# Attention and token/channel mixer on one core: Q, K and u transposed by the DMA crossbar instead of TensorE

## Chip, cores, metric

One core of a Trainium2 chip. The metric is device time in microseconds (us) of one execution; lower is better. Executions of the kernel before agree within 0.4%.

## The reference

Block-sparse attention over 4 batches x 8 heads x 768 positions x 64, then a token mixer and a channel mixer over x of 4 x 768 x 512:

```python
scores = scale * q @ k.T            # 768 x 768 per head
mask   = band | first/last block | 3 sampled blocks per row of blocks
attn   = softmax(where(mask, scores, -1e9)) @ v
x = attn, heads side by side        # B, S, 512
h = relu(x.T @ w_tok1) @ w_tok2     # along the 768 positions
u = x + h.T
out = u + relu(u @ w_ch1) @ w_ch2   # along the 512 channels, 1536 inside
```

## The kernel before

Heads go in pairs, 16 of them. A small planner inside the kernel keeps a clock for each engine, with booked costs, and writes the instructions down in the order of its plan. Each engine then runs its own list in that order and waits on semaphores. So a wait in one list stops all that stands behind it.

TensorE contracts over partitions, so Q and K (positions on partitions as loaded) must be turned, and so must u before the channel mixer. Before, both go over TensorE, PSUM and a copy:

```python
def transposes(p):                      # pair p: K, then Q
    ...
    for c in range(NC):                 # 6 chunks of 128 positions
        nc.tensor.matmul(out=box["t"][:, c, :], lhsT=lays[nm][:, c, :, :]..., rhs=ident,
                         is_transpose=True, ...)
    for hd in range(2):                 # one PSUM copy per head
        nc.vector.tensor_copy(out=buf[0:64, :], in_=i)      # or nc.scalar.copy
# rows 64 to 88 of every K and Q buffer hold the block mask; they are written once

def tok(b, g):                          # half g of the channels of batch b
    ... token mixer, u = x + h ...
    for dmc in (2 * g, 2 * g + 1):
        for sc in range(NC):
            nc.tensor.matmul(out=tbox["pt"][:, sc, :], lhsT=u[:, sc, 128 * dmc : ...],
                             rhs=ident, is_transpose=True, ...)
        nc.vector.tensor_copy(out=uT[:, dmc, :], in_=pt)    # or nc.scalar.copy

P.stream(0, qk_stream())    # scores, exponentials on ScalarE
P.stream(1, pv_stream())    # values, normalised by DVE
P.stream(2, tr_stream())    # transposes of Q and K
P.stream(3, tok_stream())
P.stream(4, ch_stream())    # channel mixer, lowest priority: fills what is left
```

Loads are issued by GpSimd, which casts float32 to bf16 on the way; Q, K and V of a pair are 128 partitions x 2 runs of 1536 bytes each.

The softmax here doesn't subtract the row's maximum and nothing guards it: scores larger than these inputs give would overflow.

## Time and profile before

| | before |
|---|---|
| time, median | 288.54 us (288.20 to 288.65, 4 runs) |
| span of the profiled run | 287.1 us |
| TensorE / ScalarE / DVE busy | 94% / 67% / 45% |
| first score matmul of pair 2 (the third pair) | 34.3 us |
| end of the last exponential | 160.9 us |
| from there to the end | 126.2 us |

The last three rows cut the span into a start, an attention stage and a channel stage.

### The profile page before, as it was taken

To read this page: it belongs to the slowest core of one execution; us is meant where nothing else is said; L and a number is where in the kernel's file an instruction comes from. 1 tells how busy PE (TensorE), PEld (TensorE's weight loads), DVE (VectorE), ACT (ScalarE), POOL (GpSimd) and SP (SyncE) were. 2 spreads that over 40 slices of the span, in tenths; PEclk is the share of its full clock that TensorE was granted. 3 is DMA by queue.
4 is the path that set the end of the run, shared out by engine and by line. 5 is a ranking of instruction groups with operands and counts; after the bars stand their busy time and mean duration, and the time that the engine had idled before them with its cause. 6 is when DMAs were issued, how large, how long until landed. Compare 5 with 4: busy or idle time off the path is not lost.

```text
span 287.1 us, 6351 instructions
## 1 busy us (share of the span) xinstructions
PE 269.9 (94%) x2682; PEld 175.5 (61%) x2690; DVE 130.2 (45%) x286; ACT 191.9 (67%) x286; POOL 45.0 (16%) x70
## 2 busy tenths in 40 slices
PE   0799899999999999999999999999999999999994
PEld 0366676678777777777777754456544654456441
DVE  5789966557777569765546341210022001200121
ACT  1589999999999999999999642037501770067200
POOL 7956554522211000000000000000000000000000
PEclk9999999999999999999999999999999999999999
DMA  4999999996254100000000001220022001210122
GB/s 55 134 204 202 214 201 205 201 185 87 39 73 66 23 2 2 0 2 3 2 0 2 2 0 39 106 76 0 2 110 84 29 0 73 94 54 0 38 102 82
DMA packets 19168, 20.07 MB, mean 70 GB/s; under 512 B 1348, under 2 KB 15428, under 8 KB 19140
## 3 DMA queue, kind: packets, MB, share of 16 engines
q0 software_dynamic: 15648, 13.37, 30.3%
q1 hardware_dynamic: 3492, 6.29, 5.8%
q8 instruction: 21, 0.34, 0.5%
q14 instruction: 7, 0.06, 0.1%
HBM read 26.74 MB, written 6.29 MB: 115 GB/s over the span
## 4 chain that ended last, share of the span: by engine, by line
PE 73%; ACT 14%; DVE 6%; issue 2%; DMA 2%; POOL 2%; POOLq 0%; DVEq 0%; ACTq 0%
PE pm_ch L686 22%; PE pm_ch L664 21%; ACT et L478 14%; PE ps L470 14%; PE po L520 8%; PE pm_tok L578 3%; PE pm_tok L603 2%; DMA kraw<-in_k_dram 2%; DVE qtb L439 1%; PE pm_ut L628 1%; PE tq L421 1%; DVE ktb L439 1%; PE tk L421 1%; DVE x L535 1%; DVE klay L394 1%
## 5 line engine op out<-in xcount | busy, mean ns | idle before, releaser
L478 ACT ACTIVATE et<-ps 128x768 bf16<-128x768 f32 x192 | 143.2, 810 | 4.2 <-PE ps L470 3.2
L470 PE MATMUL ps<-qtb,ktb 88*128 88x384 bf16 x384 | 95.3, 329 | 4.0 <-ACT et L478 1.7
L560 ACT ACTIVATE rc<-pm_ch 128x384 bf16<-128x384 f32 x84 | 41.2, 491 | 60.7 <-PE pm_ch L664 44.8
L520 PEld LDWEIGHTS <-et 128*128 128x128 bf16 x1152 | 56.0, 97 | 22.8 <-DVE x L535 1.9
L664 PE MATMUL pm_ch<-uT,w_ch 128*128 128x384 bf16 x384 | 68.6, 326 | 0.2 <-DVE rc L562 0.2
L686 PE MATMUL pm_ch<-w_ch,rc 128*128 128x512 bf16 x280 | 62.4, 379 | 0.4
L520 PE MATMUL po<-vaug,et 128*128 128x65 bf16 x1152 | 61.5, 193 | 0.5 <-ACT et L478 0.2
L694 DVE TENSOR_TENSOR o<-pm_ch,x 128x512 f32<-128x512 f32 x24 | 16.6, 692 | 98.7 <-PE pm_ch L686 98.7
L664 PEld LDWEIGHTS <-w_ch 128*128 128x128 bf16 x384 | 37.0, 98 | 23.1 <-issue 0.3
L686 PEld LDWEIGHTS <-rc 128*128 128x128 bf16 x288 | 28.2, 98 | 33.6
L470 PEld LDWEIGHTS <-ktb 88*128 88x128 bf16 x384 | 34.2, 99 | 11.9 <-issue 4.4
L439 DVE COPY ktb<-tk 64x768 bf16<-64x768 bf16 x29 | 16.0, 552 | 17.5 <-PE tk L421 17.2
L611 DVE TENSOR_TENSOR x<-pm_tok,x 128x512 bf16<-128x512 f32 x24 | 16.2, 687 | 6.8 <-PE pm_tok L603 6.5
L535 DVE TENSOR_TENSOR x<-po,recip 128x384 bf16<-128x384 f32 x32 | 17.8, 557 | 1.1
L439 DVE COPY qtb<-tq 64x768 bf16<-64x768 bf16 x30 | 16.6, 552 | 2.1 <-PE tq L421 1.1
L603 PE MATMUL pm_tok<-a_t,w_tok 128*128 128x256 bf16 x96 | 17.0, 272 | 0.0
L230 POOL DMA_DIRECT2D vraw<-in_v_dram x16 | 12.3, 766 | 28.4 <-DVE vaug L391 25.7
L578 PE MATMUL pm_tok<-x,w_tok 128*128 128x256 bf16 x96 | 16.3, 272 | 0.0
L230 POOL DMA_DIRECT2D kraw<-in_k_dram x16 | 11.6, 727 | 7.7 <-DVE recip L534 2.2
L230 POOL DMA_DIRECT2D qraw<-in_q_dram x16 | 11.5, 720 | 6.4 <-DMA w_ch<-in_moe_w_ch_dram 2.4
L534 DVE RECIPROCAL recip<-po 128x6 f32<-128x6 f32 x32 | 6.2, 195 | 12.0 <-PE po L520 11.6
L421 PE MATMUL tq<-ident,qlay 128*128 128x128 bf16 x96 | 11.3, 230 | 0.2 <-DVE qlay L394 0.2
(49 smaller groups left out, 122.8 us busy)
## 6 DMA issues: line engine op xcount, KB each, us to landing
out_dram<-o SPq DMA_DIRECT2D x24, 256.0 KB, 2.0
kraw<-in_k_dram POOLq DMA_DIRECT2D x16, 192.0 KB, 7.9
qraw<-in_q_dram POOLq DMA_DIRECT2D x16, 192.0 KB, 7.4
vraw<-in_v_dram POOLq DMA_DIRECT2D x16, 192.0 KB, 7.0
w_ch<-in_moe_w_ch_dram POOLq DMA_DIRECT2D x8, 384.0 KB, 9.8
w_tok<-in_moe_w_tok_dram POOLq DMA_DIRECT2D x1, 384.0 KB, 7.8
w_tok2r<-in_moe_w_tok_dram POOLq DMA_DIRECT2D x1, 384.0 KB, 9.0
samp<-in_sampled_blocks_dram SPq DMA_DIRECT2D x1, 0.6 KB
```

The costliest lines, as they stand in the source:

```text
L230: nc.gpsimd.dma_start(out=raw[:, :, :, :], in_=APx(src, 2 * p * S * D, [[NC * D, 128], [S * D, 2], [1, NC * D]]),)
L421: nc.tensor.matmul(out=box["t"][:, c, :], lhsT=lays[nm][:, c, :, :].rearrange("p h d -> p (h d)"), rhs=ident[:, :], start=(c == 0), stop=( ...
L439: nc.vector.tensor_copy(out=buf[0:64, :], in_=i)
L470: nc.tensor.matmul(out=ps[:, hd, 0:384], lhsT=ktb[n][0:88, 128 * j : 128 * j + 128], rhs=qtb[n][0:88, 384 * half : 384 * half + 384], star ...
L478: nc.scalar.activation(out=et[:, :, :], in_=ps[:, :, 0:384], func=AF.Exp, scale=0.125)
L520: nc.tensor.matmul(out=po[:, hd, c, :], lhsT=et[:, hd, 128 * c : 128 * c + 128], rhs=va[:, hd, j, 0:65], start=(j == 0 and hd == 0 and c = ...
L535: nc.vector.tensor_tensor(out=free(xs[b][:, 3 * half, 128 * pb : 128 * pb + 128], 0, [[64, 2], [DM, 3], [1, 64]]), in0=po[:, :, :, 0:64], ...
L560: nc.scalar.activation(out=o(), in_=i, func=AF.Relu)
L578: nc.tensor.matmul(out=box["pm"][:, t, :], lhsT=w_tok1[:, sc, 128 * t : 128 * t + 128], rhs=xs[b][:, sc, 256 * g : 256 * g + 256], start=( ...
L603: nc.tensor.matmul(out=ubox["pm"][:, i, :], lhsT=w_tok2[:, t, 2 * s2 + i, :], rhs=a_t[:, t, :], start=(i == 0 and t == 0), stop=(i == 1 an ...
L664: nc.tensor.matmul(out=pbox["pm"][:, 0:384], lhsT=w_ch1[:, dmc, 128 * cc : 128 * cc + 128], rhs=st[b]["uT"][:, dmc, 384 * sh : 384 * sh + ...
L686: nc.tensor.matmul(out=pbox["pm"][:, :], lhsT=box["rc"][:, cc, 128 * sc : 128 * sc + 128], rhs=w_ch2[:, cc, :], start=(cc == 0), stop=(cc ...
```

## The change

The intent: take 264 transposes off TensorE and their PSUM copies off DVE, and let the DMA crossbar turn the data from SBUF to SBUF. Cut to its core:

```diff
+    NPE = 2          # pairs that stay on TensorE
+    NL = 3           # wide tiles: 64 columns of data, 24 of mask, 40 zeros per head and chunk
+    wide = {(nm, n): sb1.tile([128, 2, NC, 128], BF16, ...) for n in range(NL) for nm in ("k", "q")}
...
+    def crossbar(p):
+        lays = relayout(p)           # raw -> wide[nm, p % NL][:, :, :, 0:64]
+        for nm, bufs, there in (("k", ktb, kT_there), ("q", qtb, qT_there)):
+            nc.sync.dma_start_transpose(
+                out=bufs[p % NV][:, :, :].rearrange("e h (c s) -> e (h c) s", c=NC),
+                in_=wide[nm, p % NL][:, :, :, :].rearrange("p h c e -> p (h c e)"))
+            ev = P.op(("sp",), {"sp": 1500.0}, deps, emit, prio=1, lat=2500.0)
     def transposes(p):
+        if p >= NPE:
+            crossbar(p)
+            return
...
+        nc.sync.dma_start_transpose(      # in tok(b, g), one per half batch
+            out=st[b]["uT"][:, g, :, :, :].rearrange("e c m p -> e (c m) p"),
+            in_=st[b]["u"][:, g, :, :].rearrange("p c e -> p (c e)"))
-        for dmc in (2 * g, 2 * g + 1):    # the 12 transposes and 2 copies of u
-            ...
```

The layouts of x, u and their transpose are changed to suit, and clears and mask copies for the wide tiles come in. The planner books 1.5 us for the issue of a transpose and 2.5 us from there to its landing.

More of the change, by code (lines that the diff above doesn't have):

```diff
@@ L64, in __init__ @@
         self.now = 0.0
-        self.free_at = {"pe": 0.0, "act": 0.0, "dve": 0.0}
+        self.free_at = {"pe": 0.0, "act": 0.0, "dve": 0.0, "sp": 0.0}
         self.streams = []
@@ L75, in stream, with op @@
         self.streams.sort(key=lambda s: (s[0], s[1]))
-    def op(self, engines, cost, deps, emit, prio=5, lat=60.0):
+    def op(self, engines, cost, deps, emit, prio=5, lat=60.0, tags=()):
         done = Ev()
-        self.ops.append((prio, self.count, engines, cost, deps, emit, done, lat))
+        self.ops.append((prio, self.count, engines, cost, deps, emit, done, lat, tags))
         self.count += 1
@@ L130, in step @@
             nxt.append(self.free_at["pe"])
-        for eng in ("act", "dve"):
+        for eng in ("act", "dve", "sp"):
             if self.free_at[eng] > self.now:
@@ L136, in step @@
             for o in self.ops:
-                prio, num, engines, cost, deps, emit, done, lat = o
+                prio, num, engines, cost, deps, emit, done, lat, tags = o
                 if eng not in engines:
@@ L141, in step @@
                     continue
-                t = self.when(deps)
+                t = self.when(deps, tags)
                 if t is None:
@@ L150, in step @@
             if best is not None:
-                prio, num, engines, cost, deps, emit, done, lat = best
+                prio, num, engines, cost, deps, emit, done, lat, tags = best
                 self.ops.remove(best)
@@ L208 @@
     vaug = [sb1.tile([128, 2, NC, 66], BF16, name=f"vaug{n}") for n in range(NV)]
-    qtb = [sb1.tile([128, S], BF16, name=f"qtb{n}") for n in range(2 * NV)]
-    ktb = [sb1.tile([128, S], BF16, name=f"ktb{n}") for n in range(2 * NV)]
+    qtb = [sb1.tile([128, 2, S], BF16, name=f"qtb{n}") for n in range(NV)]
+    ktb = [sb1.tile([128, 2, S], BF16, name=f"ktb{n}") for n in range(NV)]
+    wide = {
+        (nm, n): sb1.tile([128, 2, NC, 128], BF16, name=f"{nm}wide{n}")
+        for n in range(NL) for nm in ("k", "q")
+    }
     P = Planner({"ps": 2, "po": 1, "pm": 3, "et": NET, "a_t": 2, "o": 3, "rc": 2,
-                 "lay": 2, "kq": NV, "va": NV})
+                 "uT": 3})
     US = 1e3
@@ L324 @@
     indf = ind[R, :, :].rearrange("k c p -> k (c p)")
-    rows_there = {("k", n): Ev() for n in range(2 * NV)} | {("q", n): Ev() for n in range(2 * NV)}
+    rows_there = {(nm, n): Ev() for nm in ("k", "q") for n in range(2 * NPE)}
+    wide_there = {(nm, n): Ev() for nm in ("k", "q") for n in range(NL)}
     def mask_stream():
@@ L345, in copy @@
             def copy(eng, h=h):
-                nc.scalar.copy(out=qtb[0][R, 384 * h : 384 * h + 384], in_=pms[h][R, 0:384])
+                nc.scalar.copy(
+                    out=qtb[0][R, 0, 384 * h : 384 * h + 384], in_=pms[h][R, 0:384]
+                )
             e2.append(P.op(("act",), {"act": 420.0}, [done], copy, prio=0))
@@ L349, in mask_stream @@
         rows_there["q", 0].same_as = e2[1]
-        for n in range(2 * NV):
+        for n in range(2 * NPE):
             for nm, bufs in (("k", ktb), ("q", qtb)):
@@ L356, in copy @@
                     nc.vector.tensor_copy(
-                        out=bufs[n][R, :], in_=indf if nm == "k" else qtb[0][R, :]
+                        out=bufs[n // 2][R, n % 2, :], in_=indf if nm == "k" else qtb[0][R, 0, :]
                     )
@@ L367, with wide_stream, emit, clear @@
     ones_there = [Ev() for _ in range(NV)]
+    def wide_stream():
+        box, done, rel = {}, Ev(), Ev()
+        def emit():
+            P.take("pm", rel)
+            box["m"] = psM.tile([128, 2, NC, 24], FP32, tag="pm", name="pm_wide")
+            for i, rhs in enumerate((ident[R, 64:88], t2add[R, :])):
+                for c in range(NC):
+                    nc.tensor.matmul(
+                        out=box["m"][:, i, c, :], lhsT=ind[R, c, :], rhs=rhs,
+                        start=(i == 0 and c == 0), stop=(i == 1 and c == NC - 1),
+                    )
+        yield 500.0, [Ev(12.5 * US)], [("pm", 1)], emit, done
+        for n in range(NL):
+            for i, nm in enumerate(("k", "q")):
+                def clear(eng, nm=nm, n=n):
+                    nc.vector.memset(wide[nm, n][:, :, :, 64:128], 0.0)
+                def copy(eng, nm=nm, n=n, i=i):
+                    nc.vector.tensor_copy(
+                        out=wide[nm, n][:, :, :, 64:88],
+                        in_=free(box["m"][:, i, 0, :], 0, [[0, 2], [24, NC], [1, 24]]),
+                    )
+                ev = P.op(("dve",), {"dve": 420.0}, [], clear, prio=6)
+                ev = P.op(("dve",), {"dve": 450.0}, [done, ev], copy, prio=6)
+                wide_there[nm, n].same_as = ev
+                rel.same_as = ev
     START = 6.5 * US
@@ L391, in emit @@
                     nc.vector.tensor_copy(out=vaug[p % NV][:, :, :, 0:64], in_=raw[:, :, :, :])
-                    return
-                lay = sbw.tile([128, NC, 2, D], BF16, tag=f"{nm}lay", bufs=2, name=f"{nm}lay{p}")
-                nc.vector.tensor_copy(
-                    out=lay[:, :, :, :], in_=raw[:, :, :, :].rearrange("p h c d -> p c h d")
-                )
-                lays[nm] = lay
+                elif p >= NPE:
+                    nc.vector.tensor_copy(out=wide[nm, p % NL][:, :, :, 0:64], in_=raw[:, :, :, :])
+                else:
+                    lay = sbw.tile([128, NC, 2, D], BF16, tag=f"{nm}lay", bufs=1, name=f"{nm}lay{p}")
+                    nc.vector.tensor_copy(
+                        out=lay[:, :, :, :], in_=raw[:, :, :, :].rearrange("p h c d -> p c h d")
+                    )
+                    lays[nm] = lay
             deps = [arr]
@@ L401, in relayout @@
                 deps.append(pv_done[p - NV])
-            if nm != "v" and p >= 2:
-                deps.append(qT_there[p - 2, 1])
+            if nm != "v" and 1 <= p < NPE:
+                deps.append(qT_there[p - 1, 1])
+            if nm != "v" and p >= NPE:
+                deps.append(wide_there[nm, p % NL])
+                if p - NL >= NPE:
+                    deps.append(xb_done[nm, p - NL])
             lays[nm + "ev"] = P.op(("dve",), {"dve": 320.0}, deps, emit, prio=2 if nm != "v" else 3)
@@ L407, in relayout, with emit @@
         return lays
+    xb_done = {}
+    def crossbar(p):
+        lays = relayout(p)
+        for nm, bufs, there in (("k", ktb, kT_there), ("q", qtb, qT_there)):
+            def emit(eng, nm=nm, bufs=bufs):
+                nc.sync.dma_start_transpose(
+                    out=bufs[p % NV][:, :, :].rearrange("e h (c s) -> e (h c) s", c=NC),
+                    in_=wide[nm, p % NL][:, :, :, :].rearrange("p h c e -> p (h c e)"),
+                )
+            deps = [lays[nm + "ev"]]
+            if p >= NV:
+                deps.append(qk_done[p - NV])
+            ev = P.op(("sp",), {"sp": 1500.0}, deps, emit, prio=1, lat=2500.0)
+            xb_done[nm, p] = ev
+            there[p, 0], there[p, 1] = ev, ev
     def transposes(p):
+        yield lambda: ("v", p) in raws
+        if p >= NPE:
+            crossbar(p)
+            return
         for hd in range(2):
             kT_there[p, hd], qT_there[p, hd] = Ev(), Ev()
-        yield lambda: ("v", p) in raws
         lays = relayout(p)
@@ L425, in emit, with evac @@
                     )
-                deps = [lays[nm + "ev"]]
-                if p >= NV:
-                    deps.append(qk_done[p - NV])
-                yield 56.0, deps, [("pm", 1)] if c == 0 else [], emit, last if c == NC - 1 else None
-            n_left = [2]
+                yield 56.0, [lays[nm + "ev"]], [("pm", 1)] if c == 0 else [], emit, last if c == NC - 1 else None
             for hd in range(2):
-                buf = bufs[2 * (p % NV) + hd]
-                def evac(eng, hd=hd, buf=buf, box=box):
+                def evac(eng, hd=hd, buf=bufs[p % NV], box=box):
                     i = box["t"][64 * hd : 64 * hd + 64, :, :].rearrange("p c s -> p (c s)")
                     if eng == "act":
-                        nc.scalar.copy(out=buf[0:64, :], in_=i)
+                        nc.scalar.copy(out=buf[0:64, hd, :], in_=i)
                     else:
-                        nc.vector.tensor_copy(out=buf[0:64, :], in_=i)
+                        nc.vector.tensor_copy(out=buf[0:64, hd, :], in_=i)
                 ev = P.op(("dve", "act"), {"dve": 550.0, "act": 740.0}, [last], evac, prio=2)
@@ L468, in emit @@
                 for hd in range(2):
-                    n = 2 * (p % NV) + hd
+                    n = p % NV
                     nc.tensor.matmul(
-                        out=ps[:, hd, 0:384], lhsT=ktb[n][0:88, 128 * j : 128 * j + 128],
-                        rhs=qtb[n][0:88, 384 * half : 384 * half + 384], start=True, stop=True,
+                        out=ps[:, hd, 0:384], lhsT=ktb[n][0:88, hd, 128 * j : 128 * j + 128],
+                        rhs=qtb[n][0:88, hd, 384 * half : 384 * half + 384],
+                        start=True, stop=True,
                     )
@@ L489, in qk_stream @@
                 326.0,
-                [e for hd in range(2) for e in (
-                    kT_there[p, hd], qT_there[p, hd],
-                    rows_there["k", 2 * (p % NV) + hd], rows_there["q", 2 * (p % NV) + hd],
+                [e for hd in range(2) for e in [kT_there[p, hd], qT_there[p, hd]] + (
+                    [rows_there["k", 2 * p + hd], rows_there["q", 2 * p + hd]] if p < NPE else []
                 )],
@@ L531, in norm @@
                     if b not in xs:
-                        xs[b] = sbw.tile([128, NC, DM], BF16, tag="x", bufs=B, name=f"x{b}")
+                        xs[b] = sbw.tile([128, 2, NC, 256], BF16, tag="x", bufs=B, name=f"x{b}")
                     recip = sbw.tile([128, 2, 3], FP32, tag="recip", name=f"recip{p}_{half}")
@@ L535, in norm @@
                     nc.vector.tensor_tensor(
-                        out=free(xs[b][:, 3 * half, 128 * pb : 128 * pb + 128], 0,
-                                 [[64, 2], [DM, 3], [1, 64]]),
+                        out=free(
+                            xs[b][:, pb // 2, 3 * half, 128 * (pb % 2) : 128 * (pb % 2) + 128], 0,
+                            [[64, 2], [256, 3], [1, 64]],
+                        ),
                         in0=po[:, :, :, 0:64],
@@ L579, in emit @@
                         out=box["pm"][:, t, :], lhsT=w_tok1[:, sc, 128 * t : 128 * t + 128],
-                        rhs=xs[b][:, sc, 256 * g : 256 * g + 256],
+                        rhs=xs[b][:, g, sc, :],
                         start=(t == 0 and sc == 0), stop=(t == 1 and sc == NC - 1),
@@ L585, in tok @@
         if b not in st:
-            st[b] = dict(u=xs[b], uT_there=[Ev() for _ in range(4)])
+            st[b] = dict(u=xs[b], uT_there=[Ev() for _ in range(4)], uT_rel=Ev())
         a_rel = Ev()
@@ L611, in add @@
                 nc.vector.tensor_tensor(
-                    out=st[b]["u"][:, 2 * s2 : 2 * s2 + 2, 256 * g : 256 * g + 256],
-                    in0=ubox["pm"][:, :, :],
-                    in1=xs[b][:, 2 * s2 : 2 * s2 + 2, 256 * g : 256 * g + 256], op=ALU.add,
+                    out=st[b]["u"][:, g, 2 * s2 : 2 * s2 + 2, :], in0=ubox["pm"][:, :, :],
+                    in1=xs[b][:, g, 2 * s2 : 2 * s2 + 2, :], op=ALU.add,
                 )
@@ L620, in tok, with turn @@
         alias(a_rel, last)
-        for dmc in (2 * g, 2 * g + 1):
-            last, rel, tbox = Ev(), Ev(), {}
-            for sc in range(NC):
-                def emit(sc=sc, dmc=dmc, rel=rel, tbox=tbox):
-                    if sc == 0:
-                        P.take("pm", rel)
-                        tbox["pt"] = psM.tile([128, NC, 128], BF16, tag="pm", name=f"pm_ut_{b}_{dmc}")
-                    nc.tensor.matmul(
-                        out=tbox["pt"][:, sc, :], lhsT=st[b]["u"][:, sc, 128 * dmc : 128 * dmc + 128],
-                        rhs=ident[:, :], start=(sc == 0), stop=(sc == NC - 1), is_transpose=True,
-                    )
-                yield 56.0, [u_evs[sc // 2]], [("pm", 1)] if sc == 0 else [], emit, last if sc == NC - 1 else None
-            def evac(eng, dmc=dmc, tbox=tbox):
-                if "uT" not in st[b]:
-                    st[b]["uT"] = sbw.tile([128, 4, S], BF16, tag="uT", bufs=B, name=f"uT{b}")
-                o, i = st[b]["uT"][:, dmc, :], tbox["pt"][:, :, :].rearrange("p c s -> p (c s)")
-                if eng == "act":
-                    nc.scalar.copy(out=o, in_=i)
-                else:
-                    nc.vector.tensor_copy(out=o, in_=i)
-            ev = P.op(("dve", "act"), {"dve": 555.0, "act": 740.0}, [last], evac, prio=3)
-            alias(rel, ev)
+        def turn(eng):
+            if g == 0:
+                P.take("uT", st[b]["uT_rel"])
+                st[b]["uT"] = sbw.tile([128, 2, NC, 2, 128], BF16, tag="uT", bufs=3, name=f"uT{b}")
+            nc.sync.dma_start_transpose(
+                out=st[b]["uT"][:, g, :, :, :].rearrange("e c m p -> e (c m) p"),
+                in_=st[b]["u"][:, g, :, :].rearrange("p c e -> p (c e)"),
+            )
+        ev = P.op(("sp",), {"sp": 1500.0}, u_evs, turn, prio=2, lat=2500.0,
+                  tags=[("uT", 1)] if g == 0 else [])
+        for dmc in (2 * g, 2 * g + 1):
             alias(st[b]["uT_there"][dmc], ev)
@@ L665, in emit @@
                             out=pbox["pm"][:, 0:384], lhsT=w_ch1[:, dmc, 128 * cc : 128 * cc + 128],
-                            rhs=st[b]["uT"][:, dmc, 384 * sh : 384 * sh + 384],
+                            rhs=st[b]["uT"][:, dmc // 2, 3 * sh : 3 * sh + 3, dmc % 2, :],
                             start=(dmc == 0), stop=(dmc == 3),
@@ L678, in ch @@
                 rc_there[cc, sh] = ev
+        alias(st[b]["uT_rel"], last)
         for sc in range(NC):
@@ L694, in fin @@
                 nc.vector.tensor_tensor(
-                    out=o[:, :], in0=pbox["pm"][:, :], in1=st[b]["u"][:, sc, :], op=ALU.add
+                    out=o[:, :].rearrange("p (g e) -> p g e", g=2),
+                    in0=pbox["pm"][:, :].rearrange("p (g e) -> p g e", g=2),
+                    in1=st[b]["u"][:, :, sc, :], op=ALU.add,
                 )
@@ L733 @@
     P.stream(-1, mask_stream())
+    P.stream(-1, wide_stream())
     tok2_op = P.op(("dve",), {"dve": 900.0}, [tok2_raw], wtok2_lay, prio=3)
```

## The prediction

> **What bounds the kernel now.** I read the page first (slices, chain, groups), then a table of stretches, then the TensorE timeline in one of them, and last the landing times of the loads.
>
> ```profile
> PE   0799899999999999999999999999999999999994
> DVE  5789966557777569765546341210022001200121
> ACT  1589999999999999999999642037501770067200
> DMA  4999999996254100000000001220022001210122
> ...
> 70.00:99.00 29.00, 28.96 (x413) 22.23 (x410) 19.76 (x45) 28.75 (x39) 5.01 (x7) 1.00 0.41 57
> 99.00:126.00 27.00, 27.00 (x378) 20.42 (x376) 19.30 (x45) 26.90 (x37) 0.00 (x0) 1.00 0.01 2
> ```
>
> One slice is 7.2 us. Up to about 160 us (attention) TensorE and ScalarE are both full: 39 exponentials in 29 us and 37 in 27 us, one per 0.73 to 0.74 us (columns of a stretch: its length, then busy us and count of PE, weight loads, DVE, ACT, POOL; then clock, DMA share, GB/s). After that only TensorE is full. DVE has room, except before 35 us. The 16 DMA engines are full until about 65 us and nearly idle afterwards.
>
> ```profile
> 106.24 0.49 PE L470 MATMUL ps<-qtb,ktb 88*128 88x384 bf16 x2
> 106.57 0.34 PE L520 MATMUL po<-vaug,et 128*128 128x65 bf16 x6
> 106.75 0.39 PE L421 MATMUL tk<-ident,klay 128*128 128x128 bf16 x4
> 106.97 0.49 PE L470 MATMUL ps<-qtb,ktb 88*128 88x384 bf16 x2
> ```
>
> This is one step of attention, 0.73 us from score matmul to score matmul: scores 0.33, values 0.18, and 0.22 us left, here filled with four transposes (0.055 us each when pipelined). The filler place holds whatever the order gives it: transposes of K, Q and u, token mixing, or channel matmuls (L664). ScalarE sets the pace, TensorE fits exactly. Work taken out of the filler therefore does not shorten a step. It shortens the kernel only if channel matmuls of the last stage move into the place.
>
> ```profile
> 189.61 15.60 PE pm_ch L664 x96
> 205.48 10.74 PE pm_ch L686 x49
> 216.27 4.48 PE pm_ch L686 x20
> ```
>
> From the chain in order of time: the last stage is TensorE alone, 15.60/96 = 0.1625 us per L664 matmul, (10.74+4.48)/72 = 0.211 per L686 one.
>
> **What the Trainium skill says.** "TensorE: Matmul & The Clock Gate", Part 4, gives about 275 ns for a TensorE transpose in a kernel, and notes that its output needs a copy out of PSUM. The trace has 230 ns as latency of one, but only 0.055 us as spacing; the copies are the 0.55 us DVE rows below. "DMA: Bandwidth & Descriptors", section "Latency and other measured facts", gives 261 GB/s for a DMA transpose with a non-contiguous middle dimension and about 350 to 400 GB/s if contiguous; nothing in this trace shows one. The same page, "Queues, rings and completion order": each DMA engine takes turns between its queues, packet by packet. So transposes share with the loads, which here read float32 at twice the 200 GB/s that they write, about 400 GB/s (the page's "Specifications" put the ceiling at 435). The TensorE page, Part 1, calls DVE's queue strictly first in, first out; nothing in the trace contradicts it, and the argument on loads below rests on it.
>
> **The change, part by part.**
>
> *Removed from TensorE.* 14 pairs x 12 = 168 transposes and 96 of u: 264 x 0.055 = 14.5 us; 12 tiny matmuls come in. In the built orders, 39 L664 matmuls stand before the last score matmul in the old kernel; in the new one 96 and 6 of the second channel layer do. After the last score matmul it thus has 57 x 0.1625 + 6 x 0.211 + 12 x 0.055 = 11.2 us less to do. That is the gain if attention keeps its pace. The old pace from the third pair on is (160.9 - 35.0)/168 = 0.750 us per step; at 0.74 another 1.7 us goes. Best case: 288.56 - 11.2 - 1.7 = 275.7 us.
>
> *Removed from DVE and ScalarE.*
>
> ```profile
> L439 DVE COPY ktb<-tk 64x768 bf16<-64x768 bf16 x29 | 16.0, 552 | 17.5 <-PE tk L421 17.2
> L421 PE MATMUL tq<-ident,qlay 128*128 128x128 bf16 x96 | 11.3, 230 | 0.2 <-DVE qlay L394 0.2
> ```
>
> Some 56 + 16 PSUM copies of 0.55 us, about 40 us, nearly all DVE's. DVE limits nothing after 35 us, so this counts early only. There the copies for pairs 2 and 3 (8 x 0.55) and their mask rows (8 x 0.37), 7.4 us, give way to six clears and six mask copies of the new wide tiles (estimate 0.4 to 0.7 us each from the memset and copy rows, 5 to 7 us). Even.
>
> *Added: 36 crossbar transposes* of 128 x 1536 bf16, 393 KB each: 28 for K and Q, 8 for u. In the steady state one pair per 8.8 us needs two, and half of one for u, so 3.5 us is allowed for each. At 261 to 400 GB/s (skill) one takes an estimated 1.0 to 1.5 us of all engines. Not a bound late, when the DMA is idle.
>
> *Early it is different.* All transposes for pairs 2 to 7 fall before 75 us, where the loads fill the DMA. Two things can wait:
> First, pair 2. Its scores began at 34.6 us before. In the new order its Q is fifth on SyncE's queue, behind K and Q of pair 3 and K of pair 4, since its wide tile is cleared last; its copy stands in DVE's order behind Q of pair 4, which landed at 26.9 us. So it is issued at about 29 us, and lands near 34 to 36: no gain, perhaps a loss of some us.
> Second, DVE's order. In the old kernel the copies of raw K and Q were held back by lay buffers and from pair 6 on came 2 to 23 us after the data. In the new order they stand as early as the data was planned to come: K and Q of pairs 6 and 7 ahead of the normalising of pair 2's second half, of 8 and 9 ahead of pair 4's first, of 10 and 11 ahead of pair 5's first. If a load is late, DVE stands at its copy, the one PSUM tile of the values is not emptied, TensorE stops, and so does attention.
>
> ```profile
> L230 POOL DMA_DIRECT2D qraw<-in_q_dram x1: 713/713/713, 46.5 to 46.5; - x1
> ...
> DMA to landing us min/median/max: 10.1/10.1/10.1
> ```
>
> Issue plus time to landing, taken so for each: Q of pair 7 landed at 43.0 us, 9 at 56.6, 11 at 62.5, without transposes. With pair 2 at 34.6 and 0.74 us a step, pair 5's first half is normalised at 34.6 + 42 x 0.74 + 1.5 = 67.2. By then 14 transposes have had their turn (K, Q of six pairs, two of u). With x us of full DMA each, Q of pair 11 comes at 62.5 + 14x, and attention is delayed by 14x - 4.7. (The places at pairs 7 and 9 give 8x - 1.6 and 11x - 2, no more.) For x = 0.98 (the loads' own 400 GB/s) that is 9.0 us, for 1.5 16.3, for 0.5 2.3. After pair 11 the loads are slow enough for the DMA to keep up.
>
> Sum for x = 0.98: 275.7 + 9.0 = 284.7 us, rounded to 285.
>
> **The rivals.**
> 1. *The transposes hide wholly*: packets of transposes slip between those of the loads at little cost. For it: the DMA share over 1 says that packets overlap in one engine, and their source is not HBM. Against it: the loads move a steady 200 GB/s at any mix, which looks like a ceiling. Then 275 to 278 us.
> 2. *The loads come late and DVE stalls*, as in my sum: 280 to 292 us.
> 3. *The transposes themselves are slow*, in issue or in transfer. At over 3.5 us each they set the pace: at 5 us, 36 x 5 = 180 us from 24 us on puts the end of attention past 195 instead of 160, and the time above 300 us. Nothing in the trace speaks against it, as there is no transpose in it; the skill's figures do.
>
> **Range and chances.** Over 2% faster means under 282.8 us, that is x below about 0.85, or rival 1; 2% slower means over 294.3, x above about 1.65, or rival 3. I give rival 1 and small x 0.42, the middle 0.38, slow transposes 0.20. Range 275 to 298 us.
>
> **What will show it.** L664 matmuls before the last score matmul: 96, and about 110 us from it to the end instead of 127.3. The K and Q transposes' time to landing: 3 to 5 us early, 3 late. DVE waits for kraw and qraw, a few us each between 40 and 75 us, where there was 0.5 in all. The DMA full until 80 us or so, not 65. Pair 2 starting at 34 to 36 us. If DVE shows no wait for loads, my second step is wrong and it is about 276; if steps after 80 us take over 0.76 us with TensorE waiting for ktb or qtb, the transposes are the bound.

## More of the kernel before

Every run here is of state fast, or a single run of a one-core program, for which no state is given.

One more line of the page of before is needed for comparison: what the DMA engines carried.

```profile
DMA packets 19168, 20.07 MB, mean 70 GB/s; under 512 B 1348, under 2 KB 15428, under 8 KB 19140
...
q0 software_dynamic: 15648, 13.37, 30.3%
```

Queue 0 is GpSimd's (loads). Few packets are under 512 bytes.

## The result, and the profile after

The changed kernel takes 330.16 us median (329.07 to 331.62, 4 runs): 14.5% slower, ratio 1.1448 with a 95% interval of 1.1395 to 1.15. Ratios are the mean time of one kernel's fast runs over that of the other's of the same rounds, so not quite the ratio of the medians quoted.

| | before | after | difference |
|---|---|---|---|
| span | 287.1 | 329.9 | +42.8 |
| first score matmul of pair 2 | 34.3 | 69.2 | +34.8 |
| from there to the end of the last exponential | 126.6 | 146.9 | +20.4 |
| from there to the end | 126.2 | 113.8 | -12.4 |

The hoped-for gain is there, in the last row. Ahead of it 55.2 us are lost, more than four times as much. The slices of the page of after (one is 8.2 us):

```profile
PE   1798000069499669979999999999999999999995
...
PEclk9999755559879959997999999999999999999999
DMA  3999999995989977995636320215101200130022
```

TensorE stands still from slice 5 to 8, then has smaller holes up to slice 18. The granted clock falls with the holes. The chain of work that ended last, in order of time (start, length, what), names them:

```profile
30.58 13.23 SPq L461
43.86 17.63 DMA ktb<-kwide
61.48 7.55 DMA qtb<-qwide
69.17 1.44 PE ps L530 x4
...
79.34 8.97 DMA uT<-x
...
108.44 9.75 DMA uT<-x
```

The SPq and DMA lines are all crossbar transposes. SyncE's timeline has each one (SPq is SyncE's queue; start, time to issue, and x2 where two are merged):

```profile
23.82 6.70 SPq L461 DMA_TRANSPOSE ktb<-kwide  x1
30.58 13.23 SPq L461 DMA_TRANSPOSE qtb<-qwide  x1
43.86 17.58 SPq L461 DMA_TRANSPOSE ktb<-kwide  x2
61.48 5.76 SPq L461 DMA_TRANSPOSE qtb<-qwide  x2
...
150.57 1.42 SPq L461 DMA_TRANSPOSE ktb<-kwide  x1
152.04 1.77 SPq L461 DMA_TRANSPOSE qtb<-qwide  x1
```

The same instruction takes 1.4 to 1.8 us late and up to 13.2 us early. The first four landed 21.3, 22.8, 19.1 and 13.6 us after their issue began. Pair 2 needs the fifth of them. And the DMA engines are not idle or slow meanwhile; two stretches of 9 us in the middle of the hole (length, busy us and count of PE, weight loads, DVE, ACT, POOL; clock, DMA share, GB/s):

```profile
44.00:53.00 9.00, 0.00 (x0) 0.00 (x0) 0.00 (x0) 0.00 (x0) 3.71 (x5) 0.50 1.25 194
53.00:62.00 9.00, 0.00 (x0) 0.00 (x0) 0.00 (x0) 0.00 (x0) 0.00 (x0) 0.50 1.23 194
```

Nothing computes, and 194 GB/s are moved. The view of the DMA for 44 to 53 us splits them by queue (packets, MB, share of engine time; queue 1 carries the transposes):

```profile
q0 software_dynamic: 1601, 1.33, 91.0%
q1 hardware_dynamic: 1597, 0.40, 33.6%
```

The two queues get one packet each in turn, but a packet of the loads has some 830 bytes as written (1.33 MB/1601) and one of the transposes some 250. That is about 148 GB/s for the loads, which had 203 in the same stretch before, and 45 for the transposes. Six transposes of 393 KB landed between 23.8 and 70.1 us, which is 51 GB/s. The page counts what they are made of:

```profile
DMA packets 75616, 34.20 MB, mean 104 GB/s; under 512 B 57797, under 2 KB 71877, under 8 KB 75589
```

36 transposes of 128 x 12 rows of 256 bytes are 55,296 packets under 512 bytes, about what came in.

My theory from this (theory 1 in the expectations): a transpose is quick alone; beside loads its small packets take turns with large ones of the load queue, so it gets few bytes for its turns. The rivals: A, the order on SyncE's queue, where Q of pair 2 stands fifth; B, transposes are slow of themselves when several are in flight; C, the crossbar, not the size of the packets, gives way to loads.

### The profile page after: what moved, and what is told of

It is laid out like the page before. It is cut to its first block, busy times and chain, and to the rows that moved or that the text cites. A ratio compares the mean times of both kernels' runs of the same rounds, so it can differ in the third digit from the quotient of the medians.

```text
span 329.9 us, 5871 instructions
## 1 busy us (share of the span) xinstructions
PE 266.0 (81%) x2429; PEld 166.9 (51%) x2438; DVE 102.5 (31%) x234; ACT 184.0 (56%) x270; POOL 45.2 (14%) x70
## 4 chain that ended last, share of the span: by engine, by line
PE 71%; DMA 16%; SPq 4%; ACT 4%; DVE 3%; issue 1%; POOL 1%; POOLq 0%; DVEq 0%; ACTq 0%
PE pm_ch L714 19%; PE pm_ch L737 19%; PE ps L530 17%; PE po L580 9%; DMA uT<-x 6%; DMA ktb<-kwide 5%; DMA qtb<-qwide 5%; SPq L461 4%; PE pm_tok L665 3%; ACT et L539 3%; PE pm_tok L640 3%; PE tk L487 0%; DVE x L673 0%; DVE x L595 0%; DVE eq L320 0%
## 5 line engine op out<-in xcount | busy, mean ns | idle before, releaser
L530 PE MATMUL ps<-qtb,ktb 88*128 88x384 bf16 x384 | 101.2, 348 | 9.3 <-DMA qtb<-qwide 4.6
L714 PE MATMUL pm_ch<-uT,w_ch 128*128 128x384 bf16 x384 | 73.7, 329 | 9.4 <-DMA uT<-x 9.4
L580 PEld LDWEIGHTS <-et 128*128 128x128 bf16 x1152 | 59.3, 100 | 27.9 <-issue 5.4
L530 PEld LDWEIGHTS <-ktb 88*128 88x128 bf16 x384 | 37.1, 103 | 60.8 <-issue 49.0
L622 ACT ACTIVATE rc<-pm_ch 128x384 bf16<-128x384 f32 x72 | 35.3, 490 | 55.9 <-PE pm_ch L714 55.8
L580 PE MATMUL po<-vaug,et 128*128 128x65 bf16 x1152 | 64.2, 197 | 2.8 <-DVE x L595 2.3
L640 PE MATMUL pm_tok<-x,w_tok 128*128 128x256 bf16 x96 | 17.1, 285 | 31.1 <-DVE x L595 31.1
L624 DVE TENSOR_SCALAR rc<-pm_ch 128x384 bf16<-128x384 f32 x24 | 13.3, 555 | 20.9 <-PE pm_ch L714 20.8
L236 POOL DMA_DIRECT2D vraw<-in_v_dram x16 | 12.4, 776 | 53.8 <-DVE vaug L430 36.9
L595 DVE TENSOR_TENSOR x<-po,recip 128x384 bf16<-128x384 f32 x32 | 17.8, 557 | 1.1
L432 DVE COPY kwide<-kraw 128x768 bf16<-128x768 bf16 x14 | 5.1, 371 | 37.1 <-DMA ktb<-kwide 37.1
L236 POOL DMA_DIRECT2D kraw<-in_k_dram x16 | 11.7, 729 | 27.4 <-DVE recip L594 12.8
L640 PEld LDWEIGHTS <-w_tok 128*128 128x128 bf16 x96 | 8.0, 101 | 2.1 <-issue 0.3
```

Source lines behind the costliest of these rows:

```text
L236: nc.gpsimd.dma_start(out=raw[:, :, :, :], in_=APx(src, 2 * p * S * D, [[NC * D, 128], [S * D, 2], [1, NC * D]]),)
L530: nc.tensor.matmul(out=ps[:, hd, 0:384], lhsT=ktb[n][0:88, hd, 128 * j : 128 * j + 128], rhs=qtb[n][0:88, hd, 384 * half : 384 * half + 38 ...
L580: nc.tensor.matmul(out=po[:, hd, c, :], lhsT=et[:, hd, 128 * c : 128 * c + 128], rhs=va[:, hd, j, 0:65], start=(j == 0 and hd == 0 and c = ...
L595: nc.vector.tensor_tensor(out=free(xs[b][:, pb // 2, 3 * half, 128 * (pb % 2) : 128 * (pb % 2) + 128], 0, [[64, 2], [256, 3], [1, 64]],), ...
L622: nc.scalar.activation(out=o(), in_=i, func=AF.Relu)
L640: nc.tensor.matmul(out=box["pm"][:, t, :], lhsT=w_tok1[:, sc, 128 * t : 128 * t + 128], rhs=xs[b][:, g, sc, :], start=(t == 0 and sc == 0) ...
```

## The experiments

### 1. No loads beside the transposes

```diff
-                load_pair(x, max(evs))          # pairs 4 to 15
+                raws[nm, x] = kept[nm, x % NR]  # use the tiles of pairs 0 to 3 again
-            nc.gpsimd.dma_start(out=w_ch1[:, i, :], ...)     # and w_ch2
+            nc.gpsimd.memset(w_ch1[:, i, :], 0.04)
```

> The changed kernel in the same order, but Q, K and V of pairs 4 to 15 are not loaded (the tiles of pairs 0 to 3 are used again) and the two channel weights are filled with constants by GpSimd: wrong on purpose, and no load is in flight after about 25 us. Theory 1 (a transpose is fast alone, 1.4 us to issue, and slow only while loads share the DMA engines): every transpose takes 1.4 to 1.8 us to issue and lands in under 5 us, pair 2 starts at 31 to 34 us, the time is 272 to 279 us. Rival A (order on the SyncE queue, Q of pair 2 fifth, and heads of queue that wait): pair 2 still late and the time above 300 us. Rival B (a transpose is slow of itself when several are in flight): the early ones still take 6 us and more each.

286.38 us, against 330.16 with the loads. Its output is wrong, which doesn't matter for the time. SyncE's timeline, the same first transposes:

```profile
26.33 1.49 SPq L458 DMA_TRANSPOSE ktb<-kwide  x1
27.89 1.84 SPq L458 DMA_TRANSPOSE qtb<-qwide  x1
29.77 3.64 SPq L458 DMA_TRANSPOSE ktb<-kwide  x2
```

Same order of the plan, same transposes, 44 us less: rivals A and B cannot carry the loss. But my number was 272 to 279, and some waits stayed: pair 2 begins at 38.8 us, and the chain of work that ended last has a further 5.4 us of u at 48 us and 5.7 us of Q of a later pair at 69 us. Landing takes 3.7 to 4.3 us (medians) even alone, and more behind another transpose, while the plan has what depends on it close behind. Experiment 6 tests this remainder.

### 2. Pair 2 first in the queue

```diff
-    wide[nm, p % NL]
+    wide[nm, (p - NPE) % NL]      # in three places
```

> Only the order: pair p uses wide tile (p-2) mod 3 instead of p mod 3, so K and Q of pair 2 are cleared, copied and transposed first. Theory 1: each of them still takes some 9 us beside the loads, so pair 2 starts at about 45 to 50 us instead of 69, but each further pair costs another 18 us of transposes while loads last, and the time is 300 to 325 us. Rival A (order is the cause): pair 2 starts at 30 to 36 us and the time falls to 275 to 290 us.

328.35 us (one look): about as before the edit. Pair 2 now starts at 51.6 us instead of 69.2, but its Q still landed 26.2 us after its issue began, and the next pair waits again until 69.95 us. The order was poor, but it is not the cause. Rival A falls.

### 3 and 4. Each half of the change alone

```diff
     # e3: u back on TensorE, K and Q by the crossbar
+    XU = ()                  # batches whose u the crossbar turns
     # e4: K and Q of all pairs on TensorE, u by the crossbar
+    NPE = 16; XU = (0, 1, 2, 3)
```

> Half of the change undone: u is transposed on TensorE as before, K and Q of pairs from the third on by the crossbar. Theory 1: pair 2 as late as in the changed kernel (about 69 us), the two waits for u of 9 to 10 us fall away, 5 us of TensorE work comes back: 312 to 325 us. If the u transposes were what holds up the queue: below 300 us.

> The other half undone: K and Q all on TensorE as before, u of all batches by the crossbar. Theory 1: the first u (near 50 us, beside loads) lands some 9 us after its issue and holds TensorE up for up to that long once, the later ones lie under slack; TensorE has 5.3 us less: 283 to 292 us, so within 2% of before. Rival B: several waits for u of 5 to 10 us each: above 295 us.

K and Q alone: 319.68 us (one look), inside what theory 1 said; pair 2 starts at 70.8 us. From there to the end of the last exponential it takes 129.4 us instead of 146.9, so most of what the change loses after pair 2 comes with u. u alone: 295.96 us (295.37 to 296.21), ratio 1.0257, interval 1.0237 to 1.0276. That is 4 us above my range for it, and just above the edge that I gave to rival B, but there is one wait and not several: the first u, issued at 40.3 us among loads, landed 14.4 us later.

```profile
54.69 0.80 PE L751 MATMUL pm_ch<-uT,w_ch 128*128 128x384 bf16 x2 [9.74 <-DMA uT<-x]
```

The two matmuls for which TensorE waited belong to the work of lowest priority. They stand in the list ahead of the next scores, so the scores wait too. After the hole the granted clock is 0.50 (55 to 60 us), and a step's two score matmuls take 0.83 us there instead of 0.48. The halves cost 31.4 and 7.6 us, together 39.0; the whole costs 41.6.

### 5. The cost by itself

A kernel with no compute: two transposes, or two plain copies of the same 393 KB inside SBUF, beside a stream of GpSimd loads in runs of a chosen length.

```python
nc.gpsimd.dma_start(out=raw[i], in_=APx(base, at, [[run, 128], [128 * run, m], [1, run]]))  # x22, 11 of the longest
nc.sync.dma_start_transpose(out=d, in_=wsrc)                 # "turn", x2
nc.sync.dma_start(out=d[:, :, 0:128], in_=wsrc[:, :, :])     # "short": 256-byte runs
nc.sync.dma_start(out=d, in_=wsrc)                           # "long": one run of 3072 bytes
```

> The disputed cost by itself, output wrong on purpose. Stages with a barrier between them: two crossbar transposes of 128 x 1536 bf16 alone; the same two beside GpSimd loads of float32 in runs of 1536 bytes (as Q, K and V), 256, 512, 3072 and 6144 bytes; then two plain copies of the same 393 KB inside SBUF beside loads in runs of 1536 bytes, in runs of 256 bytes and of 3072 bytes; and both copies alone. Theory 1a (the DMA engines take turns packet by packet, so a 256-byte packet of a transpose waits for one load packet each time): the transpose takes some 1.5 us alone, 3 us beside 256-byte runs, 8 to 10 us beside 1536, 13 to 16 us beside 3072 and over 20 us beside 6144 (unless large runs are cut); the plain copy in 256-byte runs is as slow as the transpose, in 3072-byte runs 2 to 4 us. Rival C (the crossbar itself yields to loads, or shares by bytes): the same time beside all run lengths, and both plain copies fast.

The first try (257.0 us) was spoilt: the instructions were moved between stages, so that the stage without loads met loads. The second kept the written order.

> The cost by itself again, with the written order kept: in the first try the scheduler moved loads and stores between the stages, so that the stage without loads met loads (15.8 and 20.4 us to landing), and the one named 1536 bytes met none (3.7 and 4.0). Stages in order: two transposes alone; beside loads in runs of 1536, 256, 512, 3072, 6144 bytes; two plain copies of 393 KB beside 1536-byte loads in runs of 256 bytes, then of 3072 bytes; both alone. From the first try, theory 1a (turns by packet) expects to landing of the second: alone 4 us; beside 1536 about 17 to 21; beside 256 and 512 8 to 12, less than beside 1536; beside 3072 and 6144 17 to 40; plain copy in 256-byte runs 15 to 21, in 3072-byte runs under 8. Rival C (the crossbar itself): the plain copy in 256-byte runs lands in under 8 us beside loads.

287.15 us, a time that means nothing here. The three stages that decide (a number in a name is the load's run in float32 elements, so 384 is 1536 bytes; lines: issue, then time to landing):

```profile
L88 SPq DMA_TRANSPOSE dturn384x<-wsrc x2: 4295/5860/7424, 33.5 to 37.8; - x2
DMA to landing us min/median/max: 13.2/15.1/16.9
...
L91 SPq DMA_DIRECT2D dshort384x<-wsrc x2: 693/2290/3887, 200.9 to 201.7; - x2
DMA to landing us min/median/max: 13.2/16.8/20.4
...
L93 SPq DMA_DIRECT2D dlong384x<-wsrc x2: 493/1098/1703, 231.7 to 232.2; - x2
DMA to landing us min/median/max: 8.0/8.5/8.9
```

| transfer of 393 KB | beside loads in runs of | us to landing, first and second of the two |
|---|---|---|
| transpose | none | 3.9, 4.2 |
| transpose | 256 B | 8.9, 12.5 |
| transpose | 512 B | 9.9, 12.4 |
| transpose | 1536 B | 13.2, 16.9 |
| transpose | 3072 B | 18.4, 23.3 |
| transpose | 6144 B | 20.7, 14.1 |
| plain copy, 256-byte runs | 1536 B | 13.2, 20.4 |
| plain copy, 3072-byte runs | 1536 B | 8.0, 8.9 |
| plain copy, 256-byte runs | none | 3.5, 3.7 |
| plain copy, 3072-byte runs | none | 2.6, 2.8 |

A plain copy in 256-byte pieces is as slow beside loads as a transpose (medians 16.8 and 15.1 us); in 3072-byte pieces it takes about half as long (8.5). Longer runs of the load make the first transpose of a stage slower throughout, from 8.9 to 20.7 us. The second one beside 6144 bytes, 14.1 us, is no exception: that stage has 11 loads, which had ended by 191.8 us, and from then to 194.5 us 1593 of the two transposes' 3072 packets moved. So the size of the packets on both sides sets it, and rival C falls: nothing special to the crossbar is needed.

The DMA view of stretches in which both queues had work shows the turns themselves, packets of loads against packets of the transfer: 2727 and 2739 (39 to 53 us, runs of 1536 bytes), 1998 and 1997 (143 to 159 us, 3072), 902 and 945 (178 to 191 us, 6144), and for the plain copy in 256-byte runs 2751 and 2712 (207 to 221 us). That is one for one, as in the changed kernel. Only beside runs of 256 bytes is it not so all the time (2645 and 504 from 72 to 75 us); why, stays open. Each stage was run once.

### 6. Without loads, with a later booking

```diff
-    wide[nm, p % NL] ... {"sp": 1500.0} ... lat=2500.0
+    wide[nm, (p - NPE) % NL] ... {"sp": 2000.0} ... lat=8000.0
```

> The changed kernel without the late loads once more (wrong on purpose), with 8 us instead of 2.5 booked by the planner between issue and landing of a transpose, and pair 2 first in the wide tiles. Without loads 286.4 us was measured, with waits left at pair 2 (38.8 us), u (5.4 us) and Q (5.7 us). If these come from an order planned for a landing that is too early, they go: 272 to 279 us. If they come from the queue being full of transposes, they stay: 283 us and more.

280.59 us (one look), between the two answers: 5.8 us of the remainder of experiment 1 was order, two edits together. What stays is in part the start, where transposes are needed as soon as they can be issued: pair 2 begins at 37.2 us even here, and at 34.1 us in experiment 7, which leaves the first pairs on TensorE.

### 7 and 8. The crossbar only after the loads

```diff
-    NPE = 2
+    NPE = 8                 # 10 in the other
+    XU = (1, 2, 3)          # u of batch 0 stays on TensorE
-    ... [Ev(12.5 * US)] ... # set-up of the wide tiles
+    ... [Ev(40 * US)] ...
     # booking 2 and 8 us, wide tile (p - NPE) % NL, mask rows in all four K/Q buffers
```

> A version meant to keep the gain: crossbar for K and Q of pairs 8 to 15 and u of batches 1 to 3 only, the rest on TensorE as before; the planner books 8 us instead of 2.5 from the end of issue to landing, so that copies which wait for a transpose stand later in DVE's order; wide tiles are set up after 40 us. In its built order TensorE has 105.5 us of channel work and u transposes after the last score matmul against 117.5 before. Theory 1: loads are done by 65 us, the transposes for pair 8 have until 80 us, so nothing waits: 275 to 280 us. If transposes are a burden at any time (rival B): waits of TensorE for ktb or qtb after 80 us and over 285 us.

> As the version from pair 8, but from pair 10 on: transposes start later still. 109.0 us left after the last score matmul. Theory 1: 278 to 282 us, a few us slower than from pair 8 as more stays on TensorE. If it is faster than from pair 8, pair 8 and 9 still meet the loads.

From pair 8: 276.81 us (276.63 to 276.96), ratio 0.9597, interval 0.9583 to 0.9611: 4.0% faster than before, with a correct result. From pair 10: 279.83 us, ratio 0.9703. Slices of the page of the version from pair 8, its first transpose on SyncE's timeline, and a table row for 70 to 100 us:

```profile
PE   0799999999999999999999999999999999999994
...
DMA  4999999999999999396030314410132002310122
...
61.22 1.86 SPq L462 DMA_TRANSPOSE ktb<-kwide  x1
...
70.00:100.00 30.00, 30.00 (x391) 22.23 (x390) 15.72 (x39) 29.87 (x41) 5.00 (x7) 1.00 1.26 156
```

No hole is left in TensorE, and its waits name neither Q, K nor u from the crossbar. The last exponential ends at 161.8 us (160.9 before), and from there to the end it takes 113.5 us instead of 126.2.

### 9, 10 and 11. One pair earlier, the old booking, and late u alone

```diff
+    NPE = 7                 # c7_late_pairs
-    {"sp": 2000.0} ... lat=8000.0
+    {"sp": 1500.0} ... lat=2500.0      # c8_short_booking
+    NPE = 16; XU = (1, 2, 3)           # c16_u_only_late
```

> Crossbar for K and Q from pair 7 on and u of batches 1 to 3, otherwise as from pair 8 (276.8 us). 105.5 us left after the last score matmul too, one pair less on TensorE. K and Q of pair 7 are due at about 70 us, their loads land at 42 to 43 and the loads fill the DMA until 65. Theory 1: transposes issued at 45 to 60 us take 9 to 20 us to land, just in time or a few us late: 276 to 283 us. If the loads did not matter it would be as fast as from pair 8 or 0.5 us faster.

> The version from pair 8 with the 1.5 and 2.5 us that the change booked for issue and landing, instead of 2 and 8. The order then lets copies that need a transpose's wide tile, and matmuls that need its result, stand earlier. If order waits matter beside the load contention: 278 to 283 us. If not: 276 to 277.5 us.

> Only u of batches 1 to 3 by the crossbar, all K and Q and u of batch 0 on TensorE. 112.9 us left after the last score matmul against 117.5 before. If the gain is what leaves the last stage: 288.4 - 4.6 = 283 to 285 us. With u of batch 0 as well it was 296.0, so the difference is what the first u, caught among the loads, costs.

From pair 7: 286.03 us (284.74 to 287.14), ratio 0.9913, 9 us slower than from pair 8, above what I gave. One pair more meets the loads: K and Q of pair 7 were issued at 51.7 and 55.2 us and landed after 13.8 and 15.2 us, Q at 70.4 us. From 60 to 75 us TensorE is busy for only 3.2 to 3.6 of each 5 us, at a clock of 0.62 and 0.50 in the last two of the three stretches. Its list of waits names DVE's normalising of attention (3.4 us), not Q itself; DVE in turn waits 3.9 and 3.0 us at wide tiles for K and Q transposes. The timeline of DVE shows how the two hang together, for K:

```profile
65.59 0.36 DVE L433 COPY kwide<-kraw 128x768 bf16<-128x768 bf16 x1 [3.90 <-DMA ktb<-kwide]
...
66.09 0.56 DVE L599 TENSOR_TENSOR x<-po,recip 128x384 bf16<-128x384 f32 x1
```

The normalising for which TensorE waits runs as soon as the late copy ahead of it is done.

With the short booking from pair 8: 281.86 us, ratio 0.9778, so 5 us of the gain hang on the order alone; DVE waits 7.0 us at wide tiles for Q transposes and 4.6 us for K there, with the long booking only 0.9 us, for Q. Only late u: 283.15 us, ratio 0.9816, as expected from the 4.6 us that leave the last stage. With u of batch 0 too it was 295.96, 12.8 us more; 9.7 us of that is the wait for the first u (experiment 4). Experiment 4 also booked the shorter times, so the rest is not shown to be u's.

## Why the prediction was wrong

**The gain was right.** I had 11.2 us leave the channel stage, and up to 1.7 more from the pace. The stage after the last exponential is 12.4 us shorter after the change, and in the version from pair 8 12.7 us, where the time shows it. The gain from the pace did not come: from pair 2 to the last exponential that version takes 127.7 us, against 126.6 before.

**The step that failed** is the price of a transpose beside loads: "For x = 0.98 (the loads' own 400 GB/s) that is 9.0 us, for 1.5 16.3, for 0.5 2.3." I let transposes and loads share the DMA by bytes, at 1.0 to 1.5 us for each transpose. They share by packets, as the page that I cited said, but I did not ask what a packet of each is. With 256 bytes against runs of 1536, the first six transposes took from 23.8 to 70.1 us, 7.7 us each: five to eight times my figure. Experiment 1 shows that it is the loads, experiment 5 and the packet counts (1601 and 1597 in 9 us) that it is the size of the pieces in one-for-one turns.

**The stall came in another place.** I expected DVE to stand at copies of raw Q and K for late loads, with pair 2 hardly delayed (34 to 36 us). The trace after the change has no wait of DVE for a load. Three lines of the waits of after, all engines (line, what, for whom: us in total, times, longest):

```profile
DVE kwide L432 <- DMA ktb<-kwide: 37.1, 2, 33.5
...
PE pm_tok L640 <- DVE x L595: 31.1, 1, 31.1
...
PE ps L530 <- DMA qtb<-qwide: 4.6, 1, 4.6
```

From 29.5 to 63.0 us DVE stands at a copy into a wide tile that a transpose still reads. Behind it in DVE's list stands the normalising of a finished pair (x, L595); TensorE has a token mixer matmul that needs this x ahead of the scores of pair 2 and stands still with it for 31.1 us; after that Q of pair 2 is itself 4.6 us late. In experiment 2, with another order, TensorE waits for late Q directly instead, 26.9 us in two waits, and the time is the same. So the mechanism of an in-order list that carries one wait to everything behind it was as I had it; what it waits for is a transpose and not a load, and it begins at 29.5 us, near pair 2, and not at pair 5, where I had worked it out (67.2 us). The loads slowed as well, from about 203 to 148 GB/s, but no wait of TensorE, ScalarE or DVE names a load; the transposes, at 45 GB/s, are what was waited for. The same happened later with u: matmuls of the lowest priority wait for it ahead of the scores (9.4 us in TensorE's waits, two times).

**The rivals.** Rival 1 (hidden) is false early; late it holds, as the version from pair 8 shows. Rival 2 had the right list, DVE's, but the wrong thing waited for, and too late a place. Rival 3 (slow transposes, over 300 us) had the right size, but for another reason: they are slow only in company. I tested it against a steady need of 3.5 us each, and dismissed a burden on the start because the sum by bytes was small. The range, 275 to 298 us, came out of the failed step. So did one of the signs: "if DVE shows no wait for loads" was to mean about 276 us; DVE shows none, and it is 330.

**Slips in the sums**, none of which carries the miss. "About 110 us" from the last score matmul to the end does not follow from a gain of 11.2: 127.3 - 11.2 is 116, and 115.0 was measured. Pair 2 began at 34.3 us before, not 34.6 or 35.0, so the old pace was 0.753 us per step. By the prediction's own times the places at pairs 7 and 9 give 8x - 2.0 and 11x - 1.7.

## What to carry to other kernels

When two DMA streams meet, compare their packets, not only their bytes: a transfer in pieces of 256 bytes that is on the critical path can starve beside bulk loads that are not urgent, while the DMA as a whole still moves some 194 GB/s, as here. Put crossbar transposes where the queues have drained, give what depends on them a generous lead in each in-order list, and keep the first tiles, which are needed at once, on the engine path. A gain measured at the end of a kernel can hide a new wait at its start, so split the span by stages before judging a change.

## What the Trainium skill lacked or had wrong

- "DMA: Bandwidth & Descriptors", "Rules for kernel authors", says that a transpose next to ordinary DMAs "needs nothing". The results were correct, so this holds for data; in time a transpose of 393 KB landed after 13.2 to 23.3 us beside loads in runs of 1536 and 3072 bytes, and after 3.9 to 4.2 us alone.
- The same page, "Why small descriptors are slow (HBM only)", exempts copies inside SBUF. Here one in 256-byte runs took 3.5 to 3.7 us against 2.6 to 2.8 us in 3072-byte runs, and beside loads 13.2 to 20.4 against 8.0 to 8.9 us.
- "Advanced Engine Details and Errata", "X-Bar Transpose (TRN2)", calls transposes as fast as regular DMAs and expects 350 to 400 GB/s. Without loads, the first eight in a row of experiment 1 took 15.3 us to issue (26.33 to 41.60 us), which is 206 GB/s.
- The time that SyncE spends on issuing such a transpose: "DMA: Bandwidth & Descriptors" has only a count of sequencer cycles for a large one in "previous generations", and nothing for one beside loads. Here it is 1.4 to 1.9 us when the DMA is free and up to 16.8 us beside loads (experiment 2); SyncE issues the next one only after that.
- "TensorE: Matmul & The Clock Gate", Part 4, gives the duration of a TensorE transpose (about 275 ns in a kernel; 230 here) and not the spacing of several. In a filled pipeline one takes 0.055 us, which makes the engine path much cheaper than that figure suggests.
